# Thresholded attention feeding a small mixture-of-experts attention: scores copied to SBUF by VectorE's first pass, with a new order of the instructions

## Chip, cores and metric

One Trainium2 (trn2) chip, one of its cores. The metric is the device time of one execution of the whole program in microseconds (us), the median over the runs of a kernel.

## What is computed

Two attention layers stand one behind the other. The first takes eight batches of eight heads, 576 tokens, 64 features; it keeps only the scores that lie within `tau` of the largest of their row. The second is a causal attention of four experts over the first one's output, of which each token uses its best two.

```python
# first layer, q, k, v: (8, 8, 576, 64)
scores = (q @ k.T) / 8
scores = where(scores >= max(scores) - tau, scores, -1e9)
attn = exp(scores - max(scores)); attn /= sum(attn) + 1e-9
x = attn @ v                          # -> (8, 576, 512)
# second layer, four experts e, two chosen per token
logits = x @ w_gate; w = softmax over the best two
s = causal((x @ wq[e]) @ (x @ wk[e]).T / 8)
out += w[e] * (softmax(s) @ (x @ wv[e]) @ wo[e])
```

## The kernel before, in words

The work of the first layer goes by pairs of heads: 32 pairs, each of five row tiles (`s` = 4, 0, 1, 2, 3; tiles 0 to 3 have 128 rows for each of the two heads, tile 4 holds the last 64 rows of both). `prep` loads K and Q of a pair and turns them with TensorE transposes (`ident,ki` and `ident,qi` in the trace, with the tails `tk` and `tq`), which land in PSUM and are copied by ScalarE into `kx` and `qx`. `scores` then does, for each row tile and head: a matmul of 128 by 576 scores into two PSUM banks (`banks<-kx,qx`, L575), VectorE's row maximum (`reduce`, L645), a threshold of one column on GpSimd (`col<-col,tau_n`, L637), the exponential on ScalarE from PSUM (L675), the masked product with its row sum on VectorE (`stt`, L659), which reads the scores in PSUM once more, the reciprocal of the sum (L636, L648) and the scaling on GpSimd (`pp<-pp,col`, L637). This makes 288 score tiles of 128 by 576. `transp`, `transp_tails` and `attnv` turn the result on TensorE and multiply it with V.

The second layer (`moe`) runs once per batch, behind four pairs: projections, gates, causal scores of two experts at a time (`scores2`), of which `masked_min` (L664, a custom VectorE instruction) adds the causal mask in PSUM and takes the minimum, and the exponential reads PSUM.

PSUM has eight banks. A score tile of the first layer is of the family `s` and takes two neighbouring banks; everything else is of the family `g` and takes one. A bank is free again when the last reader of its tile is done: for a score tile that is the masked product, L659.

No loop sets the order of the instructions. All operations go into a `Plan`, with a cost for each (`cost`, `run`, `matmul`). `arrange` ranks them by the place in the program plus a number from the tables `PLACE` and `PLACE_OP`, lets TensorE start up to `AHEAD` = 3 operations out of rank, hands out slots of tiles, and prints one list per engine; each engine works its list in that order. `fill` puts matmuls without use (`still`, L1165) into long planned gaps of TensorE in the first 80 us. So a different table or cost moves instructions on every engine.

Of the kernel before, what the change touches and what calls it, by code (L numbers as in the profile page):

```python
# [22 lines left out]
SLOTS = {"ki": 2, "qi": 2, "qx": 2, "kx": 2, "pp": 5, "st": 2, "vm": 2, "p2": 3, "pt": 5, "pt4": 2,  # L23
         "ptt": 2, "x": 12, "v2": 1, "q2": 2, "zt": 2, "z0": 2, "z1": 2, "pt2": 4}
PLACE = {
# [19 lines left out]
    "av1": 1.5198, "kT": -1.1766, "later": -2.409, "load": -2.2168, "perm": 3.2453, "qT": -1.1682, "qload": -2.1062,  # L45
# [5 lines left out]
}  # L51
PLACE_OP = {
    "ACT gw": 0.1748, "ACT kx": -0.3657, "ACT lg": 0.436, "ACT p2": 0.9369, "ACT pp": -0.266, "ACT pt": -2.6086,
    "ACT pt2": 0.7745, "ACT pt4": 0.0157, "ACT ptt": -3.7743, "ACT q2": -3.5984, "ACT q2d0": -2.5343,
    "ACT q2d1": -0.1661, "ACT qi": -3.6815, "ACT qx": 1.0489, "ACT tau_t": 0.1675, "ACT tq0": 1.6009, "ACT v2": 3.767,
    "ACT warm": 3.146, "ACT wkh": 2.5436, "ACT woh": -2.5484, "ACT wqh": -0.4803, "ACT wvh": 3.6375, "ACT x": -0.5738,
    "ACT z0": 1.9112, "ACT z1": -0.3273, "ACT zt": 4.0564, "DVE col": 0.6684, "DVE g": -0.0805, "DVE gate": -2.3704,
    "DVE gt": -0.2416, "DVE gw": 1.9262, "DVE lg": 0.1698, "DVE p2": 1.1878, "DVE pp": 0.0112, "DVE q2": 3.7093,
    "DVE qsc": -2.675, "DVE s": 1.8996, "DVE st": -1.5353, "DVE still": -1.4634, "DVE tau_n": 3.7129,
    "DVE v2": -0.8102, "DVE warm": -4.0314, "DVE x": 0.381, "DVE z0": 0.9412, "DVE z1": 0.6771, "DVE zt": -1.0543,  # L60
    "PE g": 0.0346, "PE s": 0.9801, "POOL col": -1.9206, "POOL ident": 2.0833, "POOL mask": 1.6402,
    "POOL mask2": 0.8472, "POOL p2": 0.1515, "POOL pp": 0.4508, "POOL q2d0": 0.1375, "POOL q2d1": -2.6765,
    "POOL st": -2.7552, "POOL tie": -1.6602, "POOL tk0": 0.3581, "POOL tk1": -3.3493, "POOL tq0": 0.9045,
    "POOL tq1": 1.9732, "POOL vtx0": 1.2246, "POOL vtx1": -1.1982, "POOL vtz0": -0.3869, "POOL vtz1": -0.531,
    "POOL wkl": -1.3291, "POOL wol": 1.8582, "POOL wql": -0.6015, "POOL wvh": -3.1776, "POOL wvl": -2.4348,
    "SP ki": 0.5207, "SP lg": 0.763, "SP out": -2.1432, "SP qi": 0.7356, "SP st": -0.842, "SP tk0": 1.6704,
    "SP tk1": -3.9139, "SP tq0": 1.8877, "SP tq1": -0.4887, "SP vm": -0.9968, "SP vtx0": -0.7429, "SP vtx1": -1.1194,
    "SP vtz0": -1.0997, "SP vtz1": 0.0673,
# [79 lines left out]
class Plan:  # L148
# [68 lines left out]
    def network(self):  # L217
# [13 lines left out]
        for g, ms in members.items():  # L231
# [5 lines left out]
            if ops[g].e == "PE":  # L237
                for n in ms:
                    done[n] = done[ms[-1]]
                mode[g] = ops[ms[0]].mode, ops[ms[-1]].mode, ops[ms[0]].enter  # L240
# [43 lines left out]
    def arrange(self):  # L284
# [72 lines left out]
        while wake:  # L357
# [26 lines left out]
            if e == 0:  # L384
# [3 lines left out]
                if mode[g][0] != tiled[0]:  # L388
                    t += mode[g][2]
# [100 lines left out]
def kernel(  # L490
# [70 lines left out]
    def matmul(o, x, y, start, stop):  # L561
        w = size(y)
        rows, cols = x.shape[0], size(x)
        half = rows == 64 or cols == 64
        if x.dtype == BF16:
            t, more, enter = 106, 145, 200
        elif x.dtype == F32:
            t, more = 4 * (w * 0.417 + 1) + 2, 165
            enter = 140 if cols == 64 else 200
        else:  # L570
            t, more, enter = max(112, w * 0.443 + 5.5), 162, 200
        if half:
# [3 lines left out]
        plan.ops[-1].enter = enter

    def transpose(o, x):
        plan.op("PE", 109, 109 + 217 + 35, [o], [x, ident], nc.tensor.transpose)
        plan.ops[-1].enter = 150  # L580
# [6 lines left out]
    def half_transpose(o, x, rows):  # L587
        plan.op("PE", 30, 30 + 217 + 35, [o], [x, ident[rows, rows]], nc.tensor.transpose)
        plan.ops[-1].enter = 150

    def cost(e, n, psum, accum=False, slow=False):
        if e == "DVE":
            return 150 + 1.045 * n + (75 if accum else 0) if slow or psum else 105 + 0.55 * n if n > 32 else 155
        if e == "ACT":
            return (165 + 0.86 * n if psum else 175 + 0.97 * n) + (110 if accum else 0)
        return 200 + (2.1 if slow else 0.95) * n

    def run(e, t, outs, ins, fn):
        t = 1.01 * t + (25 if e == "ACT" else 10)
        plan.op(e, t - {"DVE": 84, "ACT": 118, "POOL": 24}[e], t + 35, outs, ins, fn)  # L600
# [46 lines left out]
    def reciprocal(x):  # L647
        run("DVE", 160, [x], [x], lambda d, s: nc.vector.reciprocal(d, s))  # L648

    def stt(dst, a, x, b, op0, op1, accum=None):  # L650
# [9 lines left out]
        run("DVE", cost("DVE", size(dst), True, True), [dst] + ([accum] if accum is not None else []), refs, fn)  # L660
# [538 lines left out]
```

## Time and profile before

| | us |
|---|---|
| median of 3 runs (919.57 to 924.32) | 921.24 |
| the profiled execution | 927.58 |
| its span, first to last instruction | 925.8 |

The profiled execution is 1.78 us longer than its span and 0.7% longer than the median of the runs. In the rows below "busy" of an engine is the time in which it had an instruction under way; PE is TensorE's matmuls, PEld its weight loads, DVE VectorE, ACT ScalarE, POOL GpSimd. The ends of matmuls are modelled, so a busy PE need not be a fast one. A program instruction with fp32 operands appears as two matmuls in the trace.

### The profile page before, as it was taken

The numbers are of one execution on the slowest core, as the hardware profiler recorded it, in microseconds if no ns is written. First come the engines' busy times: TensorE is split into PE (matmuls) and PEld (weight loads), VectorE is DVE, ScalarE is ACT, GpSimd is POOL, SyncE is SP. The second block draws the span as 40 slices with busy tenths as digits, with TensorE's granted clock in tenths as the row PEclk, the third lists the DMA queues.
The fourth block names the chain that finished last, engine by engine and source line by source line (L and its number), as shares of the span: only waits on it lengthen the run. The fifth ranks groups of instructions, "written<-read, shape, count | busy, mean of one in ns | idle before, by whom it ended". The sixth has DMA issues, their size and how long they took to land.

```text
span 925.8 us, 29385 instructions
## 1 busy us (share of the span) xinstructions
PE 865.9 (94%) x11489; PEld 726.8 (79%) x11489; DVE 672.6 (73%) x2021; ACT 655.7 (71%) x1560; POOL 385.3 (42%) x757
## 2 busy tenths in 40 slices
PE   7888999889998899989998899988999889998998
PEld 5666888778887688778987788877888768887897
DVE  4777786777867777777768777677786776867565
ACT  5776767776778667786768757778667876777554
POOL 5655333552535335444244433444333533435201
PEclk9888999899999999999999999989999999999999
DMA  5432101121121211111121111221211120100002
GB/s 130 101 85 56 41 18 29 43 52 42 37 54 29 67 39 39 51 42 52 30 64 52 35 45 29 65 52 34 56 32 51 43 53 27 38 15 15 25 12 70
DMA packets 109643, 42.81 MB, mean 46 GB/s; under 512 B 96320, under 2 KB 104768, under 8 KB 109504
## 3 DMA queue, kind: packets, MB, share of 16 engines
q1 hardware_dynamic: 108144, 40.64, 17.1%
q8 instruction: 90, 1.47, 0.7%
q10 hardware_dynamic: 1360, 0.30, 0.2%
q14 instruction: 49, 0.40, 0.1%
HBM read 31.47 MB, written 9.44 MB: 44 GB/s over the span
## 4 chain that ended last, share of the span: by engine, by line
PE 81%; DVE 9%; ACT 5%; issue 3%; POOL 2%; DMA 0%; SPq 0%; DVEq 0%; ACTq 0%; POOLq 0%
PE banks L575 66%; PE banks L1168 15%; DVE pp L659 4%; ACT pp L675 3%; DVE col L645 3%; ACT pt L609 1%; POOL pp L637 1%; PE banks L1165 1%; ACT p L675 1%; DVE st L611 0%; DMA lg<-in_moe_w_gate_dram 0%; POOL p L637 0%; POOL col L637 0%; DVE p L637 0%; ACT kx L609 0%
## 5 line engine op out<-in xcount | busy, mean ns | idle before, releaser
L637 POOL TENSOR_SCALAR pp<-pp,col 128x576 f32<-128x576 f32 x284 | 208.4, 743 | 231.3 <-DVE col L648 165.1
L645 DVE TENSOR_REDUCE col<-banks 128x1 f32<-128x576 f32 x304 | 220.4, 753 | 84.9 <-PE banks L575 81.3
L675 ACT ACTIVATE pp<-banks,col 128x576 f32<-128x576 f32 (+2 forms) x291 | 208.8, 740 | 92.7 <-DVE col L645 90.5
L659 DVE SCALAR_TENSOR_TENSOR pp<-banks,col,pp 128x576 f32<-128x576 f32 x284 | 226.1, 814 | 39.9 <-ACT pp L675 31.8
L609 ACT ACTIVATE pt<-banks 128x512 f32<-128x512 f32 (+3 forms) x448 | 224.8, 569 | 38.5 <-PE banks L1168 34.4
L575 PE MATMUL banks<-kx,qx 64*128 64x288 f32 (+1 forms) x1280 | 213.3, 445 | 9.9 <-ACT pt L609 7.7
L575 PEld LDWEIGHTS banks<-kx,qx 64*128 64x128 f32 (+1 forms) x1280 | 120.5, 187 | 54.5 <-ACT pt L609 19.3
L575 PE MATMUL banks<-pt,vm 128*64 128x128 f32 (+1 forms) x2560 | 154.3, 264 | 0.0
L637 POOL TENSOR_SCALAR col<-col,tau_n 128x1 f32<-128x1 f32 x288 | 75.7, 265 | 180.2 <-DVE col L645 170.3
L575 PEld LDWEIGHTS banks<-pt,vm 128*64 128x64 f32 x2560 | 132.8, 138 | 15.1 <-issue 6.2
L1168 PE MATMUL banks<-ident,pp 64*128 64x64 f32 x2626 | 122.8, 237 | 6.0 <-POOL col L637 1.7
L1168 PEld LDWEIGHTS banks<-ident,pp 64*128 64x128 f32 x2626 | 103.2, 148 | 25.1 <-issue 9.7
L637 POOL TENSOR_SCALAR p<-p,col,gw 128x384 f32<-128x384 f32 (+3 forms) x116 | 70.2, 612 | 101.3 <-DVE col L648 51.6
L675 ACT ACTIVATE p<-banks,col 128x256 f32<-128x256 f32 (+4 forms) x141 | 77.9, 559 | 21.7 <-DVE col L664 15.2
L664 DVE CUSTOM_DVE_ANT_0 banks<-banks,mask 128x128 f32<-128x128 f32 (+3 forms) x128 | 61.0, 511 | 17.4 <-PE banks L575 16.4
L575 PE MATMUL banks<-wvh,x 128*128 128x260 f32 x320 | 63.4, 288 | 0.0
L609 ACT ACTIVATE x<-banks 128x256 fp32r<-128x256 f32 (+1 forms) x96 | 28.2, 329 | 39.5 <-PE banks L575 38.0
L575 PEld LDWEIGHTS banks<-wvh,x 128*128 128x128 f32 x320 | 51.1, 188 | 5.9 <-issue 5.6
L620 DVE TENSOR_TENSOR q<-banks,q 128x288 fp32r<-128x288 f32 x64 | 28.8, 451 | 34.8 <-ACT q L609 34.7
L575 PE MATMUL banks<-x,wqh 128*128 128x288 f32 x256 | 53.3, 300 | 0.0
L575 PE MATMUL banks<-x,wkh 128*128 128x288 f32 x256 | 53.1, 300 | 0.0
L575 PE MATMUL banks<-pt,v 128*64 128x128 f32 (+1 forms) x960 | 50.5, 258 | 1.6 <-ACT pt L609 1.6
(118 smaller groups left out, 1301.9 us busy)
## 6 DMA issues: line engine op xcount, KB each, us to landing
ki<-in_k_dram SPq DMA_DIRECT2D x64, 128.0 KB, 2.8
vm<-in_v_dram SPq DMA_DIRECT2D x32, 256.0 KB, 2.9
qi<-in_q_dram SPq DMA_DIRECT2D x62, 128.0 KB, 2.8
out_dram<-st SPq DMA_DIRECT2D x29, 256.0 KB, 2.0
tk<-in_k_dram SPq DMA_DIRECT2D x64, 16.0 KB, 2.4
vtz<-in_v_dram SPq DMA_DIRECT2D x64, 16.0 KB, 2.1
vtx<-in_v_dram SPq DMA_DIRECT2D x64, 16.0 KB, 2.1
out_dram<-st SPq DMA_DIRECT2D x8, 128.0 KB, 2.3
```

What stands on the lines that cost most here:

```text
L575: lambda o, x, y: nc.tensor.matmul(o, x, y, start=start, stop=stop))
L609: run(e, t, [dst], [src], lambda d, s: nc.scalar.activation(d, s, AF.Copy))
L620: lambda d, a, b: (nc.vector if e == "DVE" else nc.gpsimd).tensor_tensor(d, a, b, op=op))
L637: return m.tensor_scalar(d, s, x_, y_, op0=op0, op1=op1)
L645: lambda d, s: nc.vector.tensor_reduce(d, s, axis=axis, op=op, **({"negate": True} if negate else {})))
L659: return nc.vector.scalar_tensor_tensor(d, a_, x_, r.pop(0), op0=op0, op1=op1, **kw)
L664: lambda o, a, i, m: nc.vector.tensor_tensor_reduce(o, i, m, 1.0, 3e38, ALU.add, ALU.min, a))
L675: return nc.scalar.activation(d, s, AF.Exp, scale=scale, **kw)
L1165: nc.tensor.matmul(banks[:, n, :256], still_[:, :P], still_[:, :1].to_broadcast([P, 256]), start=True, stop=True)
L1168: o.fn(*(r.place() for r in (*o.outs, *o.ins)))
```

## The change

The first pass over a score tile is no longer a reduction but a `tensor_scalar` that multiplies by one, writes the tile to a new SBUF tile `sc` (three buffers) and accumulates the minimum (`copied_min`). The scale of Q is negated (`qsc`), so the minimum of the negated scores stands for the maximum. The exponential and the masked product read `sc`; the last reader of the two PSUM banks is now the first pass. In the second layer `masked_min` writes its masked scores into the SBUF tile `p2` and the exponential works there in place; for row tile 4 the separate addition of the mask (L620, 128x64) and the reduction become one `masked_min` of 576 columns.

The planner's costs are new, among them a table `CHANGE` of what it costs TensorE to go from one form of matmul to another (0: full array, 1: 64 columns, 2: 64 rows, 3: transpose), and the tables `PLACE` and `PLACE_OP` hold other numbers. Cut to its core:

```diff
-SLOTS = {..., "p2": 3, "pt": 5, ...}
+SLOTS = {..., "p2": 3, "sc": 3, "pt": 5, ...}
 PLACE = {
-    "kT": -1.1766, "qT": -1.1682, ... "s01": 0.3436, "s21": 1.7601, ...
+    "kT": -1.0327, "qT": -0.7341, ... "s01": 1.2216, "s21": 2.6807, ...
...
+CHANGE = ((0, 150, 205, 150), (205, 0, 205, 150), (205, 150, 0, 0), (205, 150, 60, 0))
+EXP_SB = True
...
-                if mode[g][0] != tiled[0]:
-                    t += mode[g][2]
+                t += CHANGE[tiled[0]][mode[g][0]]
...
+    def copied_min(o, s, least):
+        t = 85 + 1.07 * size(s)
+        plan.op("DVE", t, t + 170, [o, least], [s],
+                lambda o, a, i: nc.vector.tensor_scalar(o, i, 1.0, None, op0=ALU.mult, op1=ALU.min, accum_out=a))
...
-    scaled("DVE", tau_n, tau_t, -1.0, 0.0, op0=ALU.mult, op1=ALU.min)
-    scaled("DVE", qsc, tau_t, 0.0, SCALE, op0=ALU.is_ge, op1=ALU.mult)
+    scaled("DVE", tau_p, tau_t, 0.0, op0=ALU.max)
+    scaled("DVE", qsc, tau_t, 0.0, -SCALE, op0=ALU.is_ge, op1=ALU.mult)
...
-            reduce(nmx[:, js], sv, AX.XY, ALU.max, negate=True)
-            scaled("POOL", thr[:, js], nmx[:, js], -1.0, tau_n, ALU.mult, ALU.add)
+            c = halves(plan.tile("sc", [P, S], F32))
+            copied_min(c, sv, nmx[:, js])
+            scaled("POOL", thr[:, js], nmx[:, js], 1.0, tau_p, ALU.mult, ALU.add)
             e = halves(pp[:, j * S:(j + 1) * S])
-            exp(e, sv, bias=nmx[:, js])
-            stt(e, sv, thr[:, js], e, ALU.is_ge, ALU.mult, accum=ss[:, js])
+            exp(e, c if EXP_SB else sv, bias=nmx[:, js], scale=-1.0)
+            stt(e, c, thr[:, js], e, ALU.is_le, ALU.mult, accum=ss[:, js])
...
-            for j, sv in enumerate(views):
-                masked_min(sv, mask[:, SM - w:], nmx[:, j:j + 1])
...
-            edge = g[:, 1, HS - ST:HS]
-            tt("DVE", edge, edge, mask2, ALU.add)
...
-            if t == R:
-                reduce(nmx[:, :1], sv, AX.XY, ALU.min)
-            exp(p2[:, j * SM:j * SM + w] if t < R else halves(p2[:, :S]), sv, bias=nmx[:, j:j + 1],
-                accum=sm[:, j:j + 1], scale=-1.0)
+            e = p2[:, j * SM:j * SM + w] if t < R else halves(p2[:, :S])
+            masked_min(e, sv, mask[:, SM - w:] if t < R else halves(mask2), nmx[:, j:j + 1])
+            exp(e, e, bias=nmx[:, j:j + 1], accum=sm[:, j:j + 1], scale=-1.0)
```

What the new order does to the instructions is seen at two places. On TensorE, where one pair of heads follows another and the output of the tiles `zt` is computed, the order before is this (`kx,qx` are score matmuls, `ident` rows are transposes of what stands behind the comma):

```order
L575 MATMUL banks<-woh,zt_106 128x512
L575 MATMUL banks<-wol,zt_106 128x512
L575 MATMUL banks<-woh,zt_105 128x512
L575 MATMUL banks<-kx_68,qx_66 128x288 x8
L1168 MATMUL banks<-ident,ki_62 128x64
L1168 MATMUL banks<-ident,tk_181 128x64
L1168 MATMUL banks<-ident,ki_62 128x64 x6
L1168 MATMUL banks<-ident,tk_181 128x64
L1168 MATMUL banks<-ident,ki_62 128x64
L1168 MATMUL banks<-ident,qi_64 128x64 x8
L1168 MATMUL banks<-ident,tq_183 128x64 x2
L1168 MATMUL banks<-ident,pp_71 128x64 x16
```

and at the same place of the change this; the ten transposes of `ki_62` and `tk_184` stand a little ahead of these rows, with twelve transposes of `p` between:

```order
L571 MATMUL banks<-kx_67,qx_65 64x288 x4
L1161 MATMUL banks<-ident,pp_69 128x64 x16
L571 MATMUL banks<-kx_67,qx_65 128x288 x4
L571 MATMUL banks<-woh,zt_108 128x512
L571 MATMUL banks<-wol,zt_108 128x512
L571 MATMUL banks<-woh,zt_109 128x512
L571 MATMUL banks<-woh,zt_108 128x512
L571 MATMUL banks<-wol,zt_108 128x512
L571 MATMUL banks<-woh,zt_109 128x512
L1161 MATMUL banks<-ident,qi_64 128x64 x8
L1161 MATMUL banks<-ident,tq_186 128x64 x2
```

Before, two row tiles of scores (`x8`, four tiles of two banks, so all eight banks) are followed at once by the transposes of K and of Q. In the change score matmuls come four at a time, and the transposes of Q stand apart from those of K, behind other matmuls.

On VectorE, in the second layer's first half, the first pass and the masked product of one row tile stand like this before:

```order
L645 TENSOR_REDUCE col_128<-banks 128x1 x2
L611 COPY st_74<-banks 128x512
L659 SCALAR_TENSOR_TENSOR pp_72,col_126<-banks,col_133,pp_72 128x576 x2
L611 COPY st_75<-banks 128x512
L636 TENSOR_SCALAR col_126<-col_126 128x2
```

and like this in the change (line 661 is in `copied_min`, 650 in `stt`, 602 in `copy`):

```order
L661 TENSOR_SCALAR sc_83,col_127<-banks 128x576
L661 TENSOR_SCALAR sc_81,col_127<-banks 128x576
L602 COPY st_75<-banks 128x512
L650 SCALAR_TENSOR_TENSOR pp_69,col_130<-sc_83,col_129,pp_69 128x576
L650 SCALAR_TENSOR_TENSOR pp_69,col_130<-sc_81,col_129,pp_69 128x576
```

The two passes keep their places; the masked product no longer reads `banks`, and both of its wide inputs are now SBUF tiles. Over the whole program TensorE's list has 546 changes of matmul form in place of 489 (transposes and 64-row score matmuls behind each other: 195 in place of 155; all others 351 in place of 334), and 125 `still` matmuls in place of 35, all of the 90 new ones in the first attention pairs.

## Rows read from the trace of the kernel before

**Rows 1.** The page: busy us, share of the span and instructions of each engine.
```profile
PE 865.9 (94%) x11489; PEld 726.8 (79%) x11489; DVE 672.6 (73%) x2021; ACT 655.7 (71%) x1560; POOL 385.3 (42%) x757
```
**Rows 2.** The page, the chain of work that ended last, share by engine.
```profile
PE 81%; DVE 9%; ACT 5%; issue 3%; POOL 2%; DMA 0%; SPq 0%; DVEq 0%; ACTq 0%; POOLq 0%
```
**Rows 3.** Waits of TensorE's matmuls: who waited for whom, us in total, times, longest.
```profile
PE banks L1168 <- DVE pp L659: 32.0, 29, 1.9
PE banks L575 <- ACT pt L609: 9.4, 15, 1.4
```
**Rows 4.** Timeline, 278 to 306 us: start, us, engine, instruction, [idle before <-releaser].
```profile
278.89 1.24 PE L575 MATMUL banks<-kx,qx 64*128 64x288 f32 x8 [0.99 <-ACT pt L609]
...
301.56 2.21 PE L575 MATMUL banks<-kx,qx 64*128 64x288 f32 x16
...
302.83 2.09 DVE L645 TENSOR_REDUCE col<-banks 128x1 f32<-128x576 f32 x3 [0.47 <-PE banks L575]
...
304.84 0.81 DVE L659 SCALAR_TENSOR_TENSOR pp<-banks,col,pp 128x576 f32<-128x576 f32 x1
...
305.71 0.27 PE L1168 MATMUL banks<-ident,ki 64*128 64x64 f32 x1 [1.94 <-DVE pp L659]
```
**Rows 5.** Stretches: us, busy of PE, PEld, DVE, ACT, POOL, granted clock, DMA, GB/s.
```profile
0.00:80.00 80.00, 68.35 (x829) 50.07 (x829) 51.82 (x141) 54.84 (x111) 46.49 (x107) 0.87 0.42 96
112.00:871.00 759.00, 718.29 (x9768) 607.88 (x9764) 566.07 (x1708) 551.94 (x1319) 319.25 (x613) 0.97 0.16 42
390.00:398.00 8.00, 5.18 (x82) 4.27 (x84) 5.90 (x18) 6.85 (x16) 5.23 (x11) 0.84 0.18 39
414.00:422.00 8.00, 5.66 (x78) 3.57 (x77) 6.47 (x18) 6.69 (x13) 3.47 (x8) 1.00 0.20 54
871.00:926.00 55.00, 50.30 (x534) 45.41 (x530) 29.92 (x109) 27.09 (x86) 4.54 (x6) 0.99 0.12 40
```
**Rows 6.** Groups by line and shape: busy us, mean ns of one, idle before.
```profile
L659 DVE SCALAR_TENSOR_TENSOR pp<-banks,col,pp 128x576 f32<-128x576 f32 x284 | 226.1, 814 | 39.9 <-ACT pp L675 31.8 <-POOL col L637 5.5 <-issue 0.2
L645 DVE TENSOR_REDUCE col<-banks 128x1 f32<-128x576 f32 x304 | 220.4, 753 | 84.9 <-PE banks L575 81.3 <-ACT pt L609 0.9 <-ACT p L675 0.7
L637 POOL TENSOR_SCALAR pp<-pp,col 128x576 f32<-128x576 f32 x284 | 208.4, 743 | 231.3 <-DVE col L648 165.1 <-DVE col L636 32.2 <-PE banks L575 20.7
L675 ACT ACTIVATE pp<-banks,col 128x576 f32<-128x576 f32 x285 | 205.6, 744 | 92.7 <-DVE col L645 90.5 <-DVE gw L659 0.5 <-POOL col L637 0.4
```
**Rows 7.** Timeline of VectorE, 408 to 412 us: the two passes back to back.
```profile
408.82 1.42 DVE L645 TENSOR_REDUCE col<-banks 128x1 f32<-128x576 f32 x2 [0.78 <-PE banks L575]
...
410.56 0.82 DVE L659 SCALAR_TENSOR_TENSOR pp<-banks,col,pp 128x576 f32<-128x576 f32 x1
...
411.31 0.81 DVE L659 SCALAR_TENSOR_TENSOR pp<-banks,col,pp 128x576 f32<-128x576 f32 x1
```
**Rows 8.** Groups by shape: two-input VectorE work in SBUF, and a GpSimd scaling.
```profile
L637 POOL TENSOR_SCALAR p<-p,col,gw 128x512 f32<-128x512 f32 x29 | 22.3, 781 | 25.7 <-DVE col L648 25.7
...
L620 DVE TENSOR_TENSOR gate<-gate,tie 128x80 f32<-128x80 f32 x8 | 1.9, 241 | 0.0
...
L659 DVE SCALAR_TENSOR_TENSOR gw<-gate,gw 128x20 f32<-128x20 f32 x8 | 1.4, 179 | 6.0 <-ACT gw L675 6.0
```
**Rows 9.** Timeline, 904 us: VectorE and GpSimd, both working in SBUF at once.
```profile
904.09 0.55 DVE L637 TENSOR_SCALAR p<-p,col,gw 128x512 f32<-128x512 f32 x1
...
904.25 1.03 POOL L637 TENSOR_SCALAR p<-p,col,gw 128x512 f32<-128x512 f32 x1 [5.75 <-DVE col L648]
```
**Rows 10.** Groups by shape: ScalarE over 512 columns, source in PSUM and in SBUF.
```profile
L609 ACT ACTIVATE pt<-banks 128x512 f32<-128x512 f32 x288 | 157.9, 601 | 24.1 <-PE banks L1168 20.2
...
L609 ACT ACTIVATE woh<-st 128x512 fp32r<-128x512 f32 x2 | 1.3, 651 | 0.9 <-DMA st<-in_moe_wo_dram 0.9
```
**Rows 11.** Waits of TensorE's weight loads for nothing but their own issue.
```profile
PEld banks L575 <- issue: 30.6, 105, 0.4
```
**Rows 12.** The chain in order of time, its first matmuls: start, us, what.
```profile
1.15 5.42 PE banks L1165 x25
```

More of the change, by code (lines that the diff above doesn't have):

```diff
@@ L22 @@
 EPS = 1e-9
-SLOTS = {"ki": 2, "qi": 2, "qx": 2, "kx": 2, "pp": 5, "st": 2, "vm": 2, "p2": 3, "pt": 5, "pt4": 2,
+SLOTS = {"ki": 2, "qi": 2, "qx": 2, "kx": 2, "pp": 5, "st": 2, "vm": 2, "p2": 3, "sc": 3, "pt": 5, "pt4": 2,
          "ptt": 2, "x": 12, "v2": 1, "q2": 2, "zt": 2, "z0": 2, "z1": 2, "pt2": 4}
 PLACE = {
[19 rows of a table removed]
-    "av1": 1.5198, "kT": -1.1766, "later": -2.409, "load": -2.2168, "perm": 3.2453, "qT": -1.1682, "qload": -2.1062,
[5 rows of a table removed]
[19 rows of a table added]
+    "av1": 1.4444, "kT": -1.0327, "later": 1.7433, "load": -1.3911, "perm": 3.2453, "qT": -0.7341, "qload": -1.2168,
[4 rows of a table added]
@@ L58 @@
[L58 to L67, printed above, removed]
@@ new lines @@
+    "DVE gt": 1.9765, "DVE gw": 5.359, "DVE lg": 1.016, "DVE p2": 3.9028, "DVE pp": -0.5531, "DVE q2": 6.2857,
+    "DVE qsc": -2.8622, "DVE sc": -0.1035, "DVE st": -1.4447, "DVE still": -0.4814, "DVE tau_p": 0.8807,
+    "DVE v2": 2.0003, "DVE warm": 0.2939, "DVE x": 0.3195, "DVE z0": 2.2304, "DVE z1": 0.159, "DVE zt": 2.0055,
+    "PE g": -1.5017, "PE s": 1.4698, "POOL col": -3.0293, "POOL ident": 6.5183, "POOL mask": 2.2701,
+    "POOL mask2": -1.5054, "POOL p2": -1.7322, "POOL pp": 1.1515, "POOL q2d0": 1.9326, "POOL q2d1": -0.4273,
@@ new lines @@
+    "POOL st": -4.7961, "POOL tie": -4.1632, "POOL tk0": -1.7488, "POOL tk1": -4.6506, "POOL tq0": 3.2991,
+    "POOL tq1": -0.284, "POOL vtx0": 0.099, "POOL vtx1": -1.8361, "POOL vtz0": -1.5424, "POOL vtz1": -1.4797,
+    "POOL wkl": 0.1504, "POOL wol": 2.3037, "POOL wql": 1.3512, "POOL wvh": -0.2325, "POOL wvl": -5.4675,
+    "SP ki": 0.3554, "SP lg": 0.4166, "SP out": -1.7257, "SP qi": 1.0657, "SP st": 0.188, "SP tk0": 2.4441,
+    "SP tk1": -6.0235, "SP tq0": 1.1743, "SP tq1": -1.2151, "SP vm": -1.3425, "SP vtx0": -1.0912, "SP vtx1": 1.4099,
@@ L69 @@
+    "SP vtz0": -1.3099, "SP vtz1": 1.2953,
 }
@@ L239, in network @@
                     done[n] = done[ms[-1]]
[L240 removed]
+                mode[g] = ops[ms[0]].mode, ops[ms[-1]].mode
         net = {g: {} for g in members}
@@ L563, in matmul @@
         rows, cols = x.shape[0], size(x)
-        half = rows == 64 or cols == 64
+        form = 2 if rows == 64 else 1 if cols == 64 else 0
         if x.dtype == BF16:
-            t, more, enter = 106, 145, 200
+            t, more = 106, 145
         elif x.dtype == F32:
             t, more = 4 * (w * 0.417 + 1) + 2, 165
-            enter = 140 if cols == 64 else 200
         else:
-            t, more, enter = max(112, w * 0.443 + 5.5), 162, 200
-        if half:
+            t, more = max(112, w * 0.443 + 5.5), 162
+        if form:
             t /= 2
-        plan.op("PE", t, t + more + 35, [o], [x, y],
+        plan.op("PE", t, t + more + 20, [o], [x, y],
                 lambda o, x, y: nc.tensor.matmul(o, x, y, start=start, stop=stop))
[L576 to L580, printed above, removed]
+        plan.ops[-1].mode = form
     def transposed(x, y, blocks):
@@ L587, in half_transpose @@
     def half_transpose(o, x, rows):
-        plan.op("PE", 30, 30 + 217 + 35, [o], [x, ident[rows, rows]], nc.tensor.transpose)
-        plan.ops[-1].enter = 150
+        plan.op("PE", 31.4, 31.4 + 217 + 20, [o], [x, ident[rows, rows]], nc.tensor.transpose)
+        plan.ops[-1].mode = 3
     def cost(e, n, psum, accum=False, slow=False):
         if e == "DVE":
-            return 150 + 1.045 * n + (75 if accum else 0) if slow or psum else 105 + 0.55 * n if n > 32 else 155
+            return (68 + 1.05 * n + (70 if accum else 0) if slow or psum else 180 + 0.55 * n) if n > 32 else 80
         if e == "ACT":
-            return (165 + 0.86 * n if psum else 175 + 0.97 * n) + (110 if accum else 0)
-        return 200 + (2.1 if slow else 0.95) * n
+            return (50 if psum else 92) + 0.84 * n + (90 if accum else 0)
+        return 180 + (2.1 if slow else 0.95) * n
     def run(e, t, outs, ins, fn):
-        t = 1.01 * t + (25 if e == "ACT" else 10)
-        plan.op(e, t - {"DVE": 84, "ACT": 118, "POOL": 24}[e], t + 35, outs, ins, fn)
+        plan.op(e, t, t + {"DVE": 118, "ACT": 200, "POOL": 60}[e], outs, ins, fn)
     inps = lambda *xs: any(x.v.fams[0] in ("s", "g") for x in xs)
@@ L627, in scaled @@
         kx, ky = isinstance(x, Ref), isinstance(y, Ref)
-        t = cost(e, size(src), inps(src)) + (20 * kx + 80 * ky if e == "POOL" else 50 * ky)
+        t = cost(e, size(src), inps(src)) + (0 * kx + 75 * ky if e == "POOL" else 0)
         def fn(d, s, *r):
@@ L659, in fn, with masked_min @@
             return nc.vector.scalar_tensor_tensor(d, a_, x_, r.pop(0), op0=op0, op1=op1, **kw)
-        run("DVE", cost("DVE", size(dst), True, True), [dst] + ([accum] if accum is not None else []), refs, fn)
-    def masked_min(s, m, least):
-        run("DVE", cost("DVE", size(s), True, True), [s, least], [s, m],
-            lambda o, a, i, m: nc.vector.tensor_tensor_reduce(o, i, m, 1.0, 3e38, ALU.add, ALU.min, a))
+        run("DVE", cost("DVE", size(dst), True, accum is not None, True), [dst] + ([accum] if accum is not None else []), refs, fn)
+    def masked_min(o, s, m, least):
+        t = 85 + 1.07 * size(s)
+        plan.op("DVE", t, t + 170, [o, least], [s, m],
+                lambda o, a, i, m: nc.vector.tensor_tensor_reduce(o, i, m, 1.0, 3e38, ALU.add, ALU.min, a))
+    def copied_min(o, s, least):
+        t = 85 + 1.07 * size(s)
+        plan.op("DVE", t, t + 170, [o, least], [s],
+                lambda o, a, i: nc.vector.tensor_scalar(o, i, 1.0, None, op0=ALU.mult, op1=ALU.min, accum_out=a))
     def exp(dst, src, bias=None, accum=None, scale=1.0):
@@ L675, in fn @@
             return nc.scalar.activation(d, s, AF.Exp, scale=scale, **kw)
-        run("ACT", cost("ACT", n, inps(src), accum is not None) + 80, [dst] + ([accum] if accum is not None else []),
+        run("ACT", cost("ACT", n, inps(src), accum is not None) + 100, [dst] + ([accum] if accum is not None else []),
             [src] + ([bias] if bias is not None else []), fn)
```

26 lines of the change are left out of this document (11 added, 15 removed), and 47 rows, old and new, of the table PLACE.

## The prediction

> **What bounds the kernel.** I read the page first. TensorE's matmuls are under way for 865.9 us of 925.8 (94%), VectorE for 672.6, ScalarE for 655.7 [rows 1], and the chain that ended last lies on TensorE for 81% and on VectorE for 9% [rows 2]. So TensorE bounds the kernel, and a change on VectorE pays only through what TensorE waits for. The waits of its matmuls tell that: 32.0 us, in 29 pieces of 1.1 us, behind the masked product L659, and 9.4 us behind ScalarE's copies of `pt` [rows 3]. The 29 are transposes (L1168). The timeline shows one: at 305.71 the transposes of K start 1.94 us late, released by L659 [rows 4]. They read a tile loaded from HBM, so no data come from L659; what they wait for is a PSUM bank. At 301.56 TensorE filled all eight banks with score matmuls (x16), VectorE ran three first passes from 302.83, and the first masked product only from 304.84 [rows 4]. The first bank pair was read for the first time by about 303.6 and given back about 2 us later. Last I read stretches. From 112 to 871 us TensorE idles 759.0 - 718.3 = 40.7 us at a granted clock of 0.97; the loss sits in weak stretches such as 390 to 398 us (5.18 of 8 us busy, clock 0.84) and 414 to 422 us (5.66, clock 1.00) [rows 5]. There are two of these per batch of some 111 us, seven batches. In the first 80 us it idles 11.7 us at a clock of 0.87 [rows 5].
>
> **The change, part by part**, against the profiled execution of 927.6 us.
>
> *Banks given back earlier.* The last reader of a score tile becomes the first pass. The exponential (744 ns) and the product (814 ns) drop out of the bank's time [rows 6]: 1.56 us at the least, and more where they queue. That exceeds the mean wait of 1.1 us and nearly reaches the longest, 1.94. Bounds 0 (another wait takes the place) and -32.0; I take **-30**, since in the piece shown the bank would come about 2 us earlier. Next late there is ScalarE's copy of K.
>
> *Order.* Scores come four matmuls at a time in place of eight, and Q's transposes stand apart from K's, so fewer banks are wanted at once. This and the earlier banks also touch the waits for banks behind ScalarE's copies, 0.99 us at 278.89 [rows 4], 9.4 in all [rows 3]: between 0 and -9.4, I take **-5**.
>
> *Clock.* [...] 8 us x 0.16 = 1.3 us per batch, 9 in seven batches; the second stretch had 1.00 [rows 5]. Between 0 and -9 I take **-8**.
>
> *The first pass* writes 576 columns and accumulates. A reduction alone takes 0.67 us behind another (1.42 less 0.75), a product with its accumulator 0.75 (410.56 to 411.31) [rows 7]. I take the second: +0.08 x 288 = 23 us of VectorE, bounds 0 and 0.15 each. It is covered by TensorE's own work except where TensorE runs dry: the first 80 us and two stretches of 8 us per batch, 80 + 112 = 192 of 926 us, a fifth. So **+5** (0 to +9). Without that cover it would cost all 23.
>
> *The product reads two SBUF tiles*, while GpSimd scales `pp` in SBUF. The trace has one pair of wide instructions that overlap like this: while VectorE's scaling ran at 904.09, GpSimd's took 1.03 us [rows 9] against a mean of 781 ns [rows 8], 0.25 more. If a product that meets a scaling waits for its rest: scalings fill 208.4 us, 22% of the span, the rest is 0.37 us on average [rows 6], so 0.22 x 0.37 x 288 = 24 us on VectorE, a fifth of it uncovered: **+5**. Bounds 0 and +12; GpSimd itself idles over half of the time and hides its own share. [...]
>
> *The exponential reads SBUF.* Over 512 columns ScalarE took 601 ns from PSUM and 651 from SBUF [rows 10]. +50 ns on 288 exponentials and some 140 of the second layer is 21 us, a fifth uncovered: **+4** (0 to +8).
>
> *Changes of matmul form.* 40 of the 57 more are between transposes and 64-row scores, at which I found no gap of the weight loads; the other 17 cost about 0.29 us (30.6 over 105) each [rows 11]: **+4** (0 to +10).
>
> *90 more idle matmuls* cost 5.42/25 = 0.22 us each at the low clock [rows 12], 19.5 us if all stood in front of ready work, nothing where TensorE idles anyway (11.7 us, [rows 5]), and they may raise a clock of 0.87 there. I take **0**, bounds -8 and +12.
>
> *The second layer.* The separate mask addition goes and the pass of row tile 4 gets longer, the bank comes back before the exponential; no wait of weight: **0** (-4 to +2).
>
> Sum: -30 - 5 - 8 + 5 + 5 + 4 + 4 = -25, so 902.6 us for an execution like the profiled one. That one stood 0.7% above the median of its runs (927.58 to 921.24), so the median comes to 902.6 x 0.9932 = **896 us**, its own range 884 to 911.
>
> **Rivals.**
>
> *Deeper gain.* The new order fills the weak stretches entirely: all 40.7 us of idle time go and half of the clock's loss (0.03 x 759 = 23), with the +18 of costs kept: 927.6 - 40.7 - 12 + 18 = 893, less 5 if the idle matmuls mend the first 80 us: 888, or 882 as a median. For it: the score matmuls are spread more evenly. Against it: ScalarE is busy 6.85 of 8 us in such a stretch [rows 5] and gets more work.
>
> *The wait only moves.* The transposes no longer wait for banks but the next product for its scores: the chain through one tile (pass, exponential, product) gets longer, by 0.08 + 0.06 us and a collision. Half of the -43 is given back: 927.6 - 21.5 + 18 = 924, or 918 as a median: the same. For it: the transposes' copies to `kx` and the next score matmuls stand right behind the bank in the chain. Against it: the pieces shown are waits for a bank alone.
>
> *Slower: VectorE becomes the bound.* If a product with accumulation from two SBUF tiles ran at half the rate, it would need (814 - 179)/556 = 1.14 ns more for each of 576 columns [rows 6, 8], 0.66 us. VectorE would then have 672.6 + 23 + 288 x 0.66 = 886 us of work. It idles 25 us in the last 55 and 28 in the first 80 [rows 5], of which 14 stay; with some 30 for queueing that is 955, or 948 as a median. It decides from about 0.7 us more per product: from 112 to 871 us VectorE idles 193 us [rows 5], 0.77 for each of some 250 tiles, less 0.08. Against it: a two-input SBUF addition of 80 columns takes 241 ns, a product of 20 columns 179 [rows 8], about one column per ns, so two SBUF inputs alone don't halve the rate; but that product has no accumulator. [...]
>
> *Slower by its order.* The idle matmuls all delay work (+19.5), the costs stand, and half of the gain comes: 927.6 - 21 + 18 + 15 = 940, or 933 as a median.
>
> *The change doesn't do what it says* can be set aside: in the new order no exponential or product of the first layer reads a bank.
>
> **Chances.** Forecast 0.53, deeper gain 0.17, the wait moves 0.13, VectorE bound 0.10, order 0.07. Within 0.5% (916.6 to 925.8, about what a measurement of this kernel can tell from no change) lies the moving wait: 0.13. Faster 0.53 + 0.17 = 0.70, slower 0.10 + 0.07 = 0.17. The range leaves out the VectorE bound (948), and reaches below the deep gain (882) by the low ends of the costs, about 14 us, and up to the order rival (933): 868 to 936.
>
> **What would show it.** Right: the waits of L1168 behind the masked product fall from 32 us to under 5; TensorE's busy share of the weak stretches rises and the clock there is 0.95 or more; VectorE's first pass stands near 0.75 us and the product at 0.75 to 0.85; VectorE's busy time is near 700 us. Wrong: a product of over 1.2 us (half rate), GpSimd scalings well over 0.8 us, TensorE's idle time between 112 and 871 us still near 40 us with other releasers, or a first stage that ends later than before.

## The result and the profile after

The changed kernel takes **884.19 us** (median of 4 runs, 882.52 to 884.75); the kernel before, run beside it, 922.78. The ratio is 0.9574 (95% interval 0.9524 to 0.9623). The profiled execution took 884.14 us, its span is 882.4: 43.4 less than before. The medians differ by 38.6; the execution profiled before was slower than the median of its runs.

The page of the changed kernel, engines and chain (as [rows 1] and [rows 2]):

```profile
PE 846.4 (96%) x11579; PEld 715.3 (81%) x11579; DVE 692.8 (79%) x2309; ACT 660.2 (75%) x1560; POOL 425.5 (48%) x757
...
PE 60%; DVE 20%; POOL 9%; ACT 5%; issue 5%; DMA 1%; POOLq 0%; DVEq 0%; ACTq 0%
```

TensorE has 90 matmuls more and is busy for 19.5 us less; it idles 36.0 us of its span in place of 59.9. GpSimd's share of the chain rose from 2% to 9%.

What TensorE's matmuls wait for now (as [rows 3]):

```profile
PE banks L1161 <- POOL pp L628: 11.6, 18, 1.7
PE banks L571 <- DVE sc L661: 6.2, 9, 1.2
PE banks L1161 <- POOL p L628: 3.7, 9, 0.9
PE banks L1161 <- DVE sc L661: 2.2, 6, 1.1
```

The 32.0 us behind the masked product are gone. For the reader that now releases the banks (the first pass, L661) the transposes wait 2.2 us and the other matmuls 6.2 (before: `PE banks L575 <- DVE pp L659: 1.5, 4, 0.7`). Most of the transposes' wait is now for data that GpSimd's scaling has yet to deliver. The place of [rows 4], from the timeline of the changed kernel:

```profile
293.02 0.73 DVE L661 TENSOR_SCALAR_CACHE_REDUCE sc<-banks 128x576 f32<-128x576 f32 x1
...
293.68 0.75 DVE L661 TENSOR_SCALAR_CACHE_REDUCE sc<-banks 128x576 f32<-128x576 f32 x1
...
295.79 0.27 PE L1161 MATMUL banks<-ident,ki 64*128 64x64 f32 x1
...
300.87 0.81 DVE L650 SCALAR_TENSOR_TENSOR pp<-sc,col,pp 128x576 f32<-128x576 f32 x1
301.01 0.46 PE L1161 MATMUL banks<-ident,qi 64*128 64x64 f32 x8
301.05 0.76 POOL L628 TENSOR_SCALAR col<-col,tau_p 128x1 f32<-128x1 f32 x1 [0.40 <-DVE sc L661]
```

The transposes of K and of Q start without a wait. Two first passes stand 0.66 us apart, as the reductions did (0.67, [rows 7]). And a threshold of one column takes GpSimd 0.76 us while a product runs.

The seven batches from the first to the last product of the gates (`gw`), then stretches behind an idle TensorE, of the kernel before (columns as in [rows 5]):

```profile
130.98:894.47 763.49, 722.78 (x9727) 612.97 (x9724) 562.19 (x1704) 549.11 (x1320) 313.64 (x602) 0.97 0.16 41
...
390.00:394.00 4.00, 1.76 (x18) 1.07 (x18) 3.46 (x9) 3.09 (x8) 3.40 (x8) 1.00 0.00 0
394.00:398.00 4.00, 3.42 (x64) 3.20 (x66) 2.44 (x10) 3.76 (x9) 1.83 (x4) 0.68 0.35 78
398.00:402.00 4.00, 4.00 (x66) 3.33 (x68) 2.32 (x6) 2.87 (x8) 1.51 (x3) 0.89 0.35 78
...
526.00:530.00 4.00, 1.75 (x27) 1.44 (x29) 4.00 (x10) 3.25 (x7) 0.79 (x3) 0.82 0.19 45
530.00:534.00 4.00, 4.00 (x39) 2.53 (x37) 1.33 (x7) 2.73 (x6) 2.19 (x3) 0.50 0.30 66
534.00:538.00 4.00, 4.00 (x60) 3.13 (x60) 2.64 (x6) 1.48 (x2) 1.24 (x3) 0.82 0.38 86
```

The same seven batches, and the first 80 us, of the changed kernel:

```profile
0.00:80.00 80.00, 69.34 (x922) 52.45 (x923) 58.84 (x173) 54.95 (x111) 53.09 (x105) 0.98 0.42 95
...
127.56:851.49 723.93, 703.74 (x9735) 599.87 (x9732) 576.01 (x1948) 555.13 (x1326) 344.05 (x602) 1.00 0.17 43
```

Of the 43.4 us, 763.49 - 723.93 = 39.6 lie in these seven batches, at nearly the same number of matmuls (9727 and 9735). They split in two halves: idle time 40.7 to 20.2 (-20.5) and busy time 722.8 to 703.7 (-19.0) with a granted clock of 1.00 in place of 0.97. The experiments below show that the busy time is not the clock's alone. The rows of before show where the clock was lost: in the 4 us from 390 and in those from 526 TensorE idles 2.2 us, and in the 4 us behind, of which it is busy for 3.42 and 4.00, the mean granted clock is 0.68 and 0.50.

The groups by shape of the changed kernel (as [rows 6] and [rows 8]):

```profile
L650 DVE SCALAR_TENSOR_TENSOR pp<-sc,col,pp 128x576 f32<-128x576 f32 x284 | 239.8, 867 | 45.8 <-ACT pp L672 24.9 <-POOL col L628 19.5 <-ACT ptt L600 0.3
L661 DVE TENSOR_SCALAR_CACHE_REDUCE sc<-banks 128x576 f32<-128x576 f32 x288 | 207.6, 750 | 58.6 <-PE banks L571 56.4 <-ACT qx L598 0.8
L672 ACT ACTIVATE pp<-sc,col 128x576 f32<-128x576 f32 x284 | 209.8, 776 | 57.1 <-DVE sc L661 52.9 <-DVE col L639 1.2 <-POOL pp L628 0.9
L628 POOL TENSOR_SCALAR col<-col,tau_p 128x1 f32<-128x1 f32 x288 | 91.4, 321 | 116.9 <-DVE sc L661 84.2 <-DVE col L627 21.9 <-DVE col L639 10.2
L628 POOL TENSOR_SCALAR p<-p,col,gw 128x512 f32<-128x512 f32 x30 | 35.6, 1193 | 2.1 <-ACT pp L672 1.4
```

And by line, min/median/max in ns, of the changed kernel:

```profile
L650 DVE SCALAR_TENSOR_TENSOR pp<-sc,col,pp x284: 802/816/1819, 13.9 to 824.2; 128x576 f32<-128x576 f32 x142
...
L628 POOL TENSOR_SCALAR col<-col,tau_p x288: 254/265/875, 11.2 to 823.4; 128x1 f32<-128x1 f32 x144
```

A median product takes 816 ns, and so it did before (806/816/820). Only the tail is new: 284 x (867 - 814) = 15 us.

### The profile page after: what moved, and what is told of

Same layout as the page of the kernel before. It is cut to its first block, busy times and chain, and to the rows that moved or that the text cites. A ratio compares the mean times of both kernels' runs of the same rounds, so it can differ in the third digit from the quotient of the medians.

```text
span 882.4 us, 29749 instructions
## 1 busy us (share of the span) xinstructions
PE 846.4 (96%) x11579; PEld 715.3 (81%) x11579; DVE 692.8 (79%) x2309; ACT 660.2 (75%) x1560; POOL 425.5 (48%) x757
## 4 chain that ended last, share of the span: by engine, by line
PE 60%; DVE 20%; POOL 9%; ACT 5%; issue 5%; DMA 1%; POOLq 0%; DVEq 0%; ACTq 0%
PE banks L571 49%; PE banks L1161 10%; DVE pp L650 5%; DVE sc L661 5%; POOL pp L628 3%; POOL p L628 3%; DVE p L656 2%; ACT pp L672 2%; POOL col L628 2%; ACT pt L600 2%; DVE col L627 2%; DVE x L611 1%; DVE gate L611 1%; DVE col L639 1%; PE banks L1158 1%
## 5 line engine op out<-in xcount | busy, mean ns | idle before, releaser
L628 POOL TENSOR_SCALAR pp<-pp,col 128x576 f32<-128x576 f32 x284 | 213.1, 758 | 238.6 <-DVE col L639 189.1
L650 DVE SCALAR_TENSOR_TENSOR pp<-sc,col,pp 128x576 f32<-128x576 f32 x284 | 239.8, 867 | 45.8 <-ACT pp L672 24.9
L661 DVE TENSOR_SCALAR_CACHE_REDUCE sc<-banks 128x576 f32<-128x576 f32 x288 | 207.6, 750 | 58.6 <-PE banks L571 56.4
L672 ACT ACTIVATE pp<-sc,col 128x576 f32<-128x576 f32 x284 | 209.8, 776 | 57.1 <-DVE sc L661 52.9
L571 PE MATMUL banks<-kx,qx 64*128 64x288 f32 (+1 forms) x1280 | 199.4, 425 | 3.0 <-DVE sc L661 2.0
L628 POOL TENSOR_SCALAR col<-col,tau_p 128x1 f32<-128x1 f32 x288 | 91.4, 321 | 116.9 <-DVE sc L661 84.2
L571 PEld LDWEIGHTS banks<-kx,qx 64*128 64x128 f32 (+1 forms) x1280 | 108.9, 179 | 36.4 <-issue 4.9
L1161 PE MATMUL banks<-ident,pp 64*128 64x64 f32 x2624 | 117.5, 227 | 14.8 <-POOL pp L628 11.6
L628 POOL TENSOR_SCALAR p<-p,col,gw 128x384 f32<-128x384 f32 (+3 forms) x116 | 85.5, 743 | 78.4 <-DVE col L639 32.8
L672 ACT ACTIVATE p<-p,col 128x256 f32<-128x256 f32 (+4 forms) x138 | 79.4, 584 | 7.3 <-DVE col L656 7.2
L656 DVE CUSTOM_DVE_ANT_0 p<-banks,mask 128x256 f32<-128x256 f32 (+4 forms) x138 | 67.3, 510 | 10.0 <-PE banks L571 9.9
L627 DVE TENSOR_SCALAR col<-col 128x2 f32<-128x2 f32 (+1 forms) x240 | 47.0, 199 | 3.7 <-ACT pp L672 0.2
```

The lines of the kernel that those rows point to most:

```text
L627: return m.tensor_scalar(d, s, x_, None, op0=op0)
L628: return m.tensor_scalar(d, s, x_, y_, op0=op0, op1=op1)
L650: return nc.vector.scalar_tensor_tensor(d, a_, x_, r.pop(0), op0=op0, op1=op1, **kw)
L656: lambda o, a, i, m: nc.vector.tensor_tensor_reduce(o, i, m, 1.0, 3e38, ALU.add, ALU.min, a))
L661: lambda o, a, i: nc.vector.tensor_scalar(o, i, 1.0, None, op0=ALU.mult, op1=ALU.min, accum_out=a))
L672: return nc.scalar.activation(d, s, AF.Exp, scale=scale, **kw)
```

## The experiments

The question is which part carries the gain: the dataflow (who reads PSUM last), or the new order.

**Each half alone.** First the new dataflow with the old costs and tables:

```diff
 # kernel before, with sc, copied_min, the new masked_min; costs, PLACE, PLACE_OP as before
+    "DVE sc": 0.6684,
```

> New dataflow alone (first pass copies to SBUF, readers use the copy; second layer's masked pass writes SBUF), planned with the old costs and the old order tables. Theory A (the earlier bank does it): most of the gain is there, 890 to 900 us, transposes' wait behind the masked product near zero, granted clock 0.98 or more. Theory B (the new order and costs do it): within 1% of the kernel before, 913 to 925, clock near 0.96.

Measured: 916.15 us, ratio 0.9924 (0.9895 to 0.9952). TensorE's waits in it:

```profile
PE banks L1168 <- DVE sc L668: 9.4, 12, 1.2
PE banks L1168 <- POOL pp L637: 9.3, 17, 1.5
```

Its seven batches (columns as in [rows 5]), and its matmuls without use:

```profile
140.85:881.10 740.25, 711.97 (x9740) 596.77 (x9735) 574.13 (x1946) 554.43 (x1325) 361.14 (x602) 1.00 0.16 42
...
L1165 PE MATMUL banks<-still x187: 272/272/421, 1.2 to 70.0; 128*128 128x256 bf16 x187
```

The time is that of theory B, the waits and the clock are those of theory A.

Then the new costs and tables with the old dataflow:

```diff
-            copied_min(c, sv, nmx[:, js])
+            reduce(nmx[:, js], sv, AX.XY, ALU.min)
-            exp(e, c if EXP_SB else sv, ...); stt(e, c, ...)
+            exp(e, sv, ...); stt(e, sv, ...)
```

> Old dataflow (reduction, exponential and product read PSUM; masked scores of the second layer stay in PSUM), planned with the new costs and the new order tables. Theory A: 910 to 930, transposes still wait 20 us or more behind the masked product, clock near 0.96. Theory B: 885 to 900, clock 0.98 or more.

Measured: 964.71 us, ratio 1.0451 (1.0399 to 1.0504), with these waits:

```profile
PE banks L1165 <- DVE pp L650: 28.5, 30, 2.4
PE banks L571 <- DVE pp L650: 13.8, 14, 2.1
```

The second lies outside both theories, which said 930 at most. Neither half does it: alone they bring -7 and +42 us, together -39. The dataflow by itself cuts the transposes' waits for banks from 32 to 9.4 us and lifts the mean clock to 0.992, and the stretch from the first to the last gate product shrinks by 23 us (763.5 to 740.2). But the first gate product comes at 140.85 in place of 130.98; the plan has 187 matmuls without use there in place of 35, and whether these cause the delay was not tried. Under the new tables the two dataflows lie 965 - 884 = 81 us apart. That is not the dataflow's worth alone: these tables were made for the new one, and the old one is planned by them all the same.

**Costs and tables apart**, with the new dataflow:

```diff
 # a: changed kernel (new costs), PLACE and PLACE_OP of the kernel before
 # b: first experiment (old costs), PLACE and PLACE_OP of the change
```

> New dataflow and new costs, old order tables. Theory C (the new costs alone, which now tell what a change of matmul form and a result's delay take, make the order right): 885 to 895. Theory D (the tables carry the order): 908 to 920, as with the old costs.

> New dataflow and new order tables, old costs. Theory C: 905 to 920. Theory D: 885 to 895. If tables and costs only work together: above 900, like the old tables with the new costs.

Measured: 923.78 (1.0023, 0.9996 to 1.0049) and 917.11 (0.9954, 0.9925 to 0.9982). New costs without the new tables bring nothing (both theories had said under 920), new tables without the costs 0.5%; only the pair does. The seven batches with the new costs and old tables:

```profile
139.55:891.23 751.68, 715.97 (x9739) 603.22 (x9736) 571.98 (x1945) 554.96 (x1325) 353.63 (x602) 1.00 0.16 42
```

The granted clock is that of the change, 1.00, and yet the stretch is 27.8 us longer than there (723.93). A clock that has come back is not the gain by itself. And at one clock and nearly one number of matmuls TensorE is busy for 703.7, 712.0 or 716.0 us, by the order.

**Both kernels' orders disturbed alike**, by rounding each number of the tables:

```diff
-    "s00": 0.159, "s01": 1.2216, ...
+    "s00": 0.2, "s01": 1.2, ...
```

> The changed kernel with every number of its two tables of places rounded to one decimal; dataflow and costs as changed. Theory C (the gain needs the new dataflow and an order fitted to it; either alone gives little): the order is disturbed (565 changes of tile form where the change has 546), the waits for banks come back in part, 895 to 920 us. Rival (the dataflow carries the gain and the order is a detail): 880 to 890 us.

> The kernel before with every number of its two tables rounded to one decimal; dataflow and costs as before. Theory C: the old order was fitted just as closely, so the same disturbance costs it as much or more, since a late product holds the banks longer: 935 to 965 us. Rival (the old dataflow bounds the kernel at about 920 whatever the order): 918 to 928 us. The difference to the changed kernel under the same rounding is the worth of the dataflow at equal treatment: theory C says 30 to 50 us.

Measured: 954.02 (1.0311, 1.0256 to 1.0366) and 1037.33 (1.1205, 1.1136 to 1.1273): 70 us worse than the changed kernel and some 112 worse than the kernel before, more than either theory had said. From the waits of the rounded kernel before:

```profile
PE banks L1168 <- DVE pp L659: 44.4, 42, 1.9
PE banks L575 <- DVE pp L659: 14.3, 13, 2.4
```

So both orders fit their kernels closely, and a rounded table is a worse order. Rounded alike, the two kernels lie 83 us apart. That is one rounding of each, and costs and tables differ as well as the dataflow, so it doesn't price the dataflow. That the old order had been made to live with banks that come back late would explain the first experiment; it is not shown.

**The exponential from PSUM.** The bank comes back behind the exponential:

```diff
-EXP_SB = True
+EXP_SB = False
```

> The change, but the exponential reads the scores in PSUM; only the masked product reads the copy. The bank comes back one exponential (some 0.78 us) later. Theory A: a third to a half of the bank's earlier return is lost, 890 to 900, with waits for banks now behind the exponential (ACT pp). Theory B: the same as the change, 882 to 887, or better by the 0.03 us that an exponential gains from PSUM.

Measured: 895.31, ratio 0.97 (0.9652 to 0.9748), 11 us more than the change. Waits behind the exponential appear:

```profile
PE banks L1161 <- ACT pp L672: 4.9, 8, 0.9
```

Under the new tables the time follows the last reader of the bank: 884 (pass), 895 (exponential), 965 (product). As these are planned anew each time, the steps hold the order's answer too.

**The 90 idle matmuls.**

```diff
-    idle = plan.fill(1250.0, 80000.0, 9000.0, 110.0, 217.0)
+    idle = plan.fill(1250.0, 9000.0, 9000.0, 110.0, 217.0)
```

> The change with the idle matmuls of the very start only (those before 9 us of the plan); the order of all other instructions is untouched. If the 90 added idle matmuls keep the clock up in the first 80 us: granted clock of 0 to 80 us falls from 0.98 to about 0.87 and the time rises by 2 to 6 us, all of it before 112 us. If they only delay work: 1 to 5 us faster. If they stand in idle time and the clock there costs nothing: the same within 0.3%.

Measured: 882.54 (0.9556, 0.9512 to 0.9599), 1.6 us less than with them, where the runs of each spread over 1.2 and 2.2; the rest of the order is the same. The page, and the first 80 us:

```profile
PE 839.0 (95%) x11488; PEld 709.8 (81%) x11488; DVE 693.3 (79%) x2309; ACT 659.9 (75%) x1560; POOL 427.1 (48%) x757
...
0.00:80.00 80.00, 64.13 (x849) 48.46 (x849) 60.90 (x176) 55.81 (x113) 54.65 (x105) 0.91 0.43 98
```

They do lift the clock there (0.98 with them, 0.91 without), but gain nothing. This run has as many matmuls as the kernel before, 11488 against 11489, and is busy with them for 839.0 us against 865.9.

**GpSimd's scalings**, cut to two of 576 columns (the others stay unscaled), in both kernels, each in its own order:

```diff
-            scaled("POOL", p, p, ss[:, h:h + 1], 0.0, ALU.mult, ALU.add)
+            scaled("POOL", p, p, ss[:, h:h + 1], 0.0, ALU.mult, ALU.add, part=2)
```

> The change with GpSimd's 288 scalings of pp cut to two columns (the other columns stay unscaled, so this part of the computation is left out); the order of all engines is untouched. If products that meet a scaling wait for it: the masked product's mean falls from 867 ns to 820 or less, thresholds stay a little above 265 ns. If two SBUF inputs are slow in themselves: it stays near 867. Time: if collisions and scalings lie off the path, 875 to 885; TensorE waits 11.6 us for scalings in the change, so 868 to 878 if these go; under 865 only if the collisions themselves were on the path.

> The kernel before with GpSimd's 284 wide scalings of pp done on two of their 576 columns, every instruction in its old place (the other columns stay unscaled). In the changed kernel the same cut took 18 us. If GpSimd came onto the path only with the change (before, TensorE waits 32 us for the masked product and under 3 us for GpSimd): 917 to 922 us against some 922. Rival (GpSimd's scaling stood on the path all along, and the change only made it visible): 903 to 910 us.

Measured: 866.07 from the changed kernel (0.939, 0.9343 to 0.9436), 18 us less; 923.6 from the kernel before (1.0000, 0.9960 to 1.0039), nothing. In the changed kernel, cut so:

```profile
L652 DVE SCALAR_TENSOR_TENSOR pp<-sc,col,pp 128x576 f32<-128x576 f32 x284 | 228.8, 833 | 39.6 <-ACT pp L674 32.9 <-POOL col L630 4.6 <-POOL wvl L611 0.6
L630 POOL TENSOR_SCALAR pp<-pp,col 128x2 f32<-128x2 f32 x284 | 77.4, 280 | 259.0 <-DVE col L641 202.4 <-PE banks L571 20.7 <-DVE col L629 17.4
...
PE banks L1163 <- POOL pp L630: 2.3, 6, 0.7
```

and in the kernel before, cut so:

```profile
PE banks L1170 <- DVE pp L661: 34.1, 30, 1.9
```

GpSimd came onto the path only with the change; before, TensorE waited for banks whatever GpSimd did. The mean product fell from 867 to 833 ns and not to 820. The 18 us are more than the 11.6 of TensorE's waits for the scalings; what the rest is was not separated.

**The thresholds.** The product compares the exponential with exp(-tau), formed once, instead of the copy with a threshold; the 90 idle matmuls are out too. Once planned anew, once with every instruction kept in its place:

```diff
-            scaled("POOL", thr[:, js], nmx[:, js], 1.0, tau_p, ALU.mult, ALU.add)
-            stt(e, c, thr[:, js], e, ALU.is_le, ALU.mult, accum=ss[:, js])
+            stt(e, e, tau_e, e, ALU.is_ge, ALU.mult, accum=ss[:, js])
```

> The change without its added idle matmuls and without GpSimd's 288 thresholds: the masked product compares the exponential with exp(-tau), so both of its wide inputs are the same SBUF tile and a score within the exponential's rounding of the threshold may fall on the other side. Products wait 19.5 us for thresholds in the change. If that wait and the collisions with thresholds matter: 874 to 881. If TensorE's own work is all that is left: 881 to 884, as without the idle matmuls; the planner orders anew, which may cost some us.

> The changed kernel without GpSimd's 288 thresholds and without the 90 added idle matmuls, its order kept instruction by instruction; the product compares the exponential with exp(-tau), which was formed once, in place of the copy with the threshold (scores within rounding of the threshold may fall the other way). If GpSimd's queue and its meetings with VectorE stand on the path: 91 us of GpSimd's time go (thresholds of 321 ns), the waits for its scalings shrink from 15 us, the mean product falls from 867 to 825 to 850 ns, and the time to 870 to 879 us. Rival (only the 128x576 scalings count, the thresholds lie in GpSimd's idle time): 881 to 884 us. Second rival (the replanned one came out at 920 because of the new product, not of the order): over 895 us.

Measured: planned anew 919.8 (0.999, 0.9962 to 1.0018); in the kept order **872.23** (0.9432, 0.9393 to 0.9471), the fastest whole kernel here, 10.3 us below the one without idle matmuls. Expected for the first were 874 to 884. Its 919.8 was the order's, then: the same work, planned anew with the same tables, takes 47.6 us more, more than the whole gain of the change. Every experiment above that plans anew can have such a part in its time. The page of the one planned anew, then product and waits in the kept order:

```profile
PE 850.4 (92%) x11488; PEld 715.9 (78%) x11488; DVE 696.8 (76%) x2309; ACT 657.4 (71%) x1561; POOL 356.1 (39%) x469
...
L856 DVE SCALAR_TENSOR_TENSOR pp<-pp,tau_e 128x576 f32<-128x576 f32 x284 | 235.1, 855 | 31.1 <-ACT pp L672 30.0 <-POOL pp L628 0.2
...
PE banks L1173 <- POOL pp L628: 9.9, 11, 3.2
```

The mean product stays at 855 ns, where 825 to 850 was expected: thresholds caused little of its tail. What went is VectorE's idle time for a threshold (19.5 us to none) and 12 us of TensorE's idle time (880.8 - 839.0 = 41.8 with thresholds, 870.0 - 840.4 = 29.6 without).

## Why the prediction was right, and which of its terms were off

896 us was forecast, 868 to 936 as the range, and 884 came. The direction, the mechanism (banks given back earlier) and its signs in the profile came as said; the gain was 38.6 us in place of 25 (921 less 896), at the lower end of the 884 to 911 that the text calls its own range without working it out. The idle time of the seven batches fell by 20.5, near the -17 that banks, order and costs come to; the largest error is in TensorE's busy time, which stood under the clock alone. And there was luck in it: the sum takes for granted that this order fits this dataflow. The same early banks under other orders gave 916, 924 and 917 us, and no step gives a reason why this one would fit.

- **Banks, -30, and order, -5.** The wait went as forecast, 32.0 to 2.2 us for the transposes, and 9.4 behind the copies `pt` left the first places too. The fault is that two terms stand there to be added. The runs show that they depend on each other: -7 us for the dataflow alone, +42 for the order and costs alone, -39 for both. The sentence on the order looked at two places in the list; that most of the gain needs an order made for the dataflow was not seen. How the 39 divide between the two stays open, since no run gives the banks back late in the new order kept instruction by instruction.
- **What is late next.** The step named ScalarE's copy of K. It is GpSimd's scaling, 11.6 us.
- **Clock, -8: too small, by how much is open.** TensorE's busy time fell by 19 in the seven batches and, by the run with as many matmuls as before, by 865.9 - 839.0 = 27 in all. Not all of that is the clock's: two other orders with a clock of 1.00 were busy for 712.0 and 716.0 us against 722.8 before, which is 7 to 11 less, and the change's order is another 8 to 12 below them. The kernel without thresholds, planned anew, has the same 11488 matmuls at nearly the same clock (0.987 against 0.990) and is busy for 850.4 us in place of 839.0. For what the order does to busy time the forecast had no term. The step itself counted 8 us x 0.16 in one stretch of a batch and found 1.00 in the other. The stretch ended at 398 us, where the clock had not come back (0.89 for 4 us more), and the batch at 526 lost 4 x (0.18 + 0.50 + 0.18) = 3.4 us, over twice the 1.3 of the piece that was read. The sum over the batches stood in the text as 0.03 x 759 = 23, used in a rival alone; it is more than the busy time that came back. That the clock's loss goes with the idle time was the author's estimate, and no run shows it. They show a clock of 0.97 at 40.7 us of idle time in the seven batches (before), and of 1.00 at 35.7 (new costs, old tables) and at 20.2 (the change); and within the kernel before 0.68 and 0.50 over the 4 us behind 2.2 us of idling, but 1.00 from 414 to 422 us with 2.3 us idle [rows 5].
- **First pass, +5.** Passes stand 0.66 to 0.68 us apart, not 0.75, and take 750 ns against 753: the copy costs VectorE next to nothing over the reduction. The row taken (the product's 0.75) was the wrong neighbour; the lower bound was right.
- **Collisions, +5.** They are there: 15 us on VectorE against the 24 worked out. Of the 288 products of the change 249 take at most 821 ns. The other 39 take 853 to 1819, and each of them began while a GpSimd instruction was under way and ended 0.60 to 0.62 us after that one. It goes the other way too: of the 32 thresholds over 300 ns 31 began inside a product and ended 0.13 us after it, as the one at 301.05 did (301.81 against 301.68). Before, 105 products began beside a GpSimd instruction, and none took over 820 ns. A product and the scalings beside it, of which the first ends at 277.89:

  ```profile
  277.14 1.96 POOL L628 TENSOR_SCALAR pp<-pp,col 128x576 f32<-128x576 f32 x2 [0.48 <-DVE col L639]
  ...
  277.21 1.28 DVE L650 SCALAR_TENSOR_TENSOR pp<-sc,col,pp 128x576 f32<-128x576 f32 x1 [0.26 <-ACT pp L672]
  ```

  The step's sentence that GpSimd "hides its own share" failed: the 288 thresholds went from 265 ns (75.7 us in all before) to 321, the gated scalings of 512 columns from 781 to 1193, and GpSimd's queue is on the path now. Collisions and plain load are not told apart by the cut to two columns, which takes both away.
- **Exponential, +4.** 776 against 744 ns, +32 and not +50; too little to see in the time.
- **Idle matmuls, 0.** 1.6 us, within the spread of the runs: as taken. The 0.22 us is that of the first 25 (5.42 us); five from 8.07 us took 0.73. The step's low clock is the 0.87 of the first 80 us as a whole; from 1 to 10 us of the kernel before the granted clock was 1.00. **Changes of form, +4**, and the **second layer, 0**, were not tried by themselves. By the text's own numbers 17 changes at 0.29 us are 5, not 4.
- **What would show it.** Right: the transposes' waits for banks (2.2 us), the clock (1.00), the first pass (750 ns), VectorE's busy time (692.8 us), a first gate product that comes earlier (127.56 in place of 130.98). Not as said: the product, 867 ns in the mean against 0.75 to 0.85 us; and the gated scalings over 0.8 us, named as a sign of being wrong, came without undoing the gain.
- **Rivals.** The deeper gain gave 882, nearest to the result, but by another split: half of the idle time went and nearly all of the clock's loss, where it had all and half. *The wait only moves* and *slower by its order* each have a grain of truth in the experiments (GpSimd's scaling; +42 for the order alone). The latter names +19.5 for the idle matmuls and adds 15; with 19.5 it gives 938, not 933. *VectorE becomes the bound* is refuted: no run shows the half rate, and the median product takes 816 ns from two SBUF tiles with accumulation, as from PSUM.

## What to carry to other kernels

Ask for a scarce buffer who its last reader is, and let the earliest operation that must touch the data copy it out; but judge such a change with an order fitted to it. The same edit brought 7 us under the old tables, and planning one kernel anew cost 47.6, more than the whole gain; an edit that keeps every instruction in its place tells what it is worth. Where a busy engine's clock falls behind its idle time (here to 0.68 and 0.50 over the 4 us behind 2.2 us of idling), price an idle stretch by the clock of the time after it as well; mean clock x whole stretch gave 23 us here, and no more than 19 of busy time came back, some of it by the order. Once one wait is gone, test the next one by a cut in the kernel before and in the one after: the same cut gave nothing in the one and 18 us in the other.

## What was not expected of the hardware

- A VectorE pass over 576 fp32 columns in PSUM that also writes them to SBUF stands nearly as close behind its predecessor as a reduction that writes one column: 0.66 to 0.68 us against 0.67.
- A GpSimd instruction on one column (265 ns in the median) took up to 875 ns, and a masked product of 816 up to 1819. All 39 slow products, and 31 of the 32 slow thresholds, began while the other engine was at work in SBUF, and ended a fixed 0.60 to 0.62 us, or 0.13, after it was done.
- The mean granted clock was 0.50 over 4 us in which TensorE was busy without a break, behind 4 us in which it had idled for 2.2.
- With the granted clock at 1.00 and nearly the same number of matmuls, TensorE was busy for 703.7, 712.0 or 716.0 us, by the order of its list.
